# A linear-attention and token-mixing kernel whose whole schedule is written out in tables: all tables replaced, and zero products moved to the common pool of PSUM banks

## The chip, the cores and the metric

The kernel runs on one core of one Trainium2 chip. The metric is the device time of one execution in microseconds (us). Runs of one kernel agree within about 0.2%.

The engines are named as the profile names them: PE (TensorE, matrix products; PEld its weight loads), DVE (VectorE), ACT (ScalarE), POOL (GpSimd), SP (SyncE, which only issues DMAs here). DMAs are issued by SP, by ACT and by POOL, and run on 16 DMA engines.

## What is computed

```python
# attention, 4 batches, 8 heads, 768 steps, head size 48
for t in range(S):
    cur = np.einsum('bhd,bhe->bhde', u[None] * kt, vt)
    y[:, :, t] = np.einsum('bhd,bhde->bhe', rt, state + cur)
    state = w[None, :, :, None] * state + np.einsum('bhd,bhe->bhde', kt, vt)
# mixer on x = y as (4, 768, 384)
h = np.maximum(xt @ w_tok1, 0.0) @ w_tok2     # xt: steps and channels swapped; 256 hidden
u = x + h.transpose(0, 2, 1)
out = u + np.maximum(u @ w_ch1, 0.0) @ w_ch2  # 1536 hidden
```

All inputs and the output are float32; the products run in bfloat16 with float32 sums.

## The kernel before

**Chunks.** Each batch's 768 steps are cut into six chunks of 128. For a chunk, k and r are scaled by powers of the decay (tables `wnat`, `wp`, `wpair`, made once on ACT), turned (k on PE or by a DMA transpose; r in a "window" of two chunks for batches 0 and 1), and multiplied to scores `at_ps`. DVE masks the scores into `AT` (two masks of 128x512 a chunk). PE adds `AT` times v, and r times the state so far, in `y_ps`; the term of u (the "own" term: u*k*r summed per head into `adg`, times v) is added at the end, and the result goes to `x_b`. The state moves on in `kv_ps` and `S`. Batches 2 and 3 take their four inputs' products and the own term on POOL alone, five operations a chunk.

**Mixer.** When a batch's six chunks are in `x_b`, one task takes the hidden products `h_ps<-x_b,wtok`; then come the way back (`hT_ps`, or `hx_ps` with a turn on PE for three of the first four half batches), the turned `uT`, 24 "up" products `z_ps` (two half batches of 12, three products of 384 columns each), a relu each into `zr` on ACT or DVE, and "down" products `h_ps<-wch,zr`, in tasks of four, whose sums go to `osb` and are stored. The MLP of one batch is the work that PE does while the attention of the next batch is prepared on the other engines.

**Weights.** Seven loads by POOL, with a cast to bfloat16: w0 (`w_tok1`), w1 (`w_tok2`), w2 (the first third of `w_ch1`, for up products 0 to 3 of 12), w3 (the other two thirds, of double size), w4, w5, w6 (thirds of `w_ch2`).

**What sets the order.** Nothing is decided at run time. `add` (L208 and on, class `Plan`) numbers 908 tasks in the order in which the code creates them; `Plan.run` (L233) emits them in the order of `ORDER` (L21). Each engine works its own tasks in just that order (`InOrder`, L276; this is why the profile gives L282 to nearly every instruction), and waits in place for what a task needs. So the tables fix:

- `ORDER`: the queue of each engine, SP's and POOL's DMAs too;
- `BUFS` (L62): which buffer each tile takes; `m` are the seven PSUM banks of the common pool, `kv` the eighth;
- `ENGINES` (L151): for each task that can run on two engines, which one;
- `W_DEP` (L162): weight load i is issued only after a named load of (batch, chunk, input) landed; input 0 is k, 1 is r (of two chunks in batches 0 and 1), 2 is v;
- `HOLD` (L163): a load waits for another load's landing, which limits how many are under way; `GATES` (L176): a load waits for the landing of a weight load;
- `NWARM` (L177), `FILL` (L181): products with a zero tile `warm`, whose result nobody uses. Twelve of 512 columns are tasks of their own (`keep_warm`, L1189) and write the `kv` bank; five more are put by `fill` (L308) in front of the products of four tasks, in the bank which that task is about to fill.

Tasks that the text below speaks of: 44 (`t_uw`, L465: u times ones at 8 partitions, after two small DMAs on ACT, 4 and 5; PE's `turn_u`, 45, needs it); 28 to 36 and 50 to 52 (decay tables on ACT, L444); 16 and 17 (`mask2`, `place`); 119 to 125 (w0 to w6); 255 (the first up product); 333 on (batch 1), 531 on (batch 2), 711 on (batch 3); 774 and 782 (r products of batch 3's chunks 4 and 5, after whose transposes, 775 and 783 on SP, PE takes the scores, 785); 796 (the hidden products of batch 3).

Of the kernel before, what the change touches and what calls it, by code (L numbers as in the profile page):

```python
# [60 lines left out]
]  # L61
BUFS = {  # L62
    'AT0': [
    0, 1, 2, 0, 1, 0, 2, 1, 0, 2, 1, 0, 2, 1, 0, 1, 2, 1, 0, 2, 1, 0, 2, 1,
],
    'AT1': [
    0, 1, 2, 0, 1, 0, 2, 1, 0, 2, 0, 1, 2, 1, 0, 1, 2, 0, 1, 2, 0, 1, 2, 0,
# [8 lines left out]
    0, 0, 0, 0,  # L76
],
    'adg': [
    0, 1, 2, 3, 4, 1, 0, 2, 3, 4, 1, 0, 2, 3, 4, 0, 1, 2, 3, 0, 4, 1, 2, 3,
],  # L80
    'h1r': [
    0, 1, 0, 1,
# [41 lines left out]
    0, 1, 2, 3, 4, 0, 1, 2, 3, 0, 4, 2,  # L124
],
    'uT': [
    0, 1, 2, 3, 1, 0, 3, 2,
],
    'u_sb': [
    0, 1, 2, 3, 0,  # L130
# [1104 lines left out]
```

## Time and profile before

| | us |
|---|---|
| median of 3 runs | 163.41 (163.26 to 163.44) |
| the profiled execution | 163.55 |
| its span, from the first to the last instruction | 161.8 |
| PE, DVE, ACT, POOL busy in the span | 153.7, 114.1, 68.3, 85.7 |
| products PE `h_ps<-wch,zr` x300 | 54.0 |
| products PE `z_ps<-uT,wch` x288 | 52.0 |
| zero products `kv_ps<-warm` x12 | 5.2 |

The busy time of PE is that of overlapping products, whose ends are modelled. The chain of work that ended last follows the last instruction back to what released it, step by step. In rows of waits, the columns are the time in total, the number and the longest; in timelines, start, length, engine, operation, and in brackets the idle time before with what ended it.

### The profile page before, as it was taken

The numbers are of one execution on the slowest core, as the hardware profiler recorded it, in microseconds if no ns is written. First come the engines' busy times: TensorE is split into PE (matmuls) and PEld (weight loads), VectorE is DVE, ScalarE is ACT, GpSimd is POOL, SyncE is SP. The second block draws the span as 40 slices with busy tenths as digits, with TensorE's granted clock in tenths as the row PEclk, the third lists the DMA queues.
The fourth block names the chain that finished last, engine by engine and source line by source line (L and its number), as shares of the span: only waits on it lengthen the run. The fifth ranks groups of instructions, "written<-read, shape, count | busy, mean of one in ns | idle before, by whom it ended". The sixth has DMA issues, their size and how long they took to land.

```text
span 161.8 us, 3784 instructions
## 1 busy us (share of the span) xinstructions
PE 153.7 (95%) x1459; PEld 102.2 (63%) x1459; DVE 114.1 (70%) x243; ACT 68.3 (42%) x153; POOL 85.7 (53%) x108
## 2 busy tenths in 40 slices
PE   6998789899999899999999999999999999999992
PEld 1465567567666677666677765677666666666671
DVE  6689874568888998598799927967899245743423
ACT  3989785727732441246146341046541202242200
POOL 7149892008581179999959895999924000000000
PEclk9999999999999999999999999999999999999999
DMA  4999899998989899999999799898990143500133
GB/s 126 202 205 182 138 236 222 209 231 165 231 153 221 177 203 175 239 199 145 199 237 203 173 234 169 169 233 177 170 267 21 48 88 131 150 26 0 44 142 106
DMA packets 93061, 26.89 MB, mean 166 GB/s; under 512 B 87794, under 2 KB 92148, under 8 KB 93044
## 3 DMA queue, kind: packets, MB, share of 16 engines
q1 hardware_dynamic: 90688, 23.40, 70.6%
q0 software_dynamic: 2160, 3.15, 11.3%
q8 instruction: 11, 0.18, 0.5%
q10 hardware_dynamic: 196, 0.11, 0.2%
q14 instruction: 6, 0.05, 0.1%
HBM read 20.46 MB, written 4.72 MB: 156 GB/s over the span
## 4 chain that ended last, share of the span: by engine, by line
PE 65%; DMA 22%; DVE 3%; ACT 3%; SPq 2%; issue 1%; POOL 1%; POOLq 0%
PE h_ps L282 30%; PE z_ps L282 24%; DMA wch<-in_moe_w_ch_dram 9%; DMA kt<-in_k_dram 8%; DMA vt<-in_v_dram 5%; PE hT_ps L282 3%; PE y_ps L282 3%; PE at_ps L282 3%; SPq L282 2%; DVE AT L282 2%; PE kv_ps L282 1%; PE hx_ps L282 1%; DVE S L282 1%; ACT vb L282 1%; POOL kr L282 1%
## 5 line engine op out<-in xcount | busy, mean ns | idle before, releaser
L282 PE MATMUL h_ps<-wch,zr 128*128 128x384 bf16 (+1 forms) x300 | 54.0, 319 | 0.7 <-DMA wch<-in_moe_w_ch_dram 0.5
L282 PE MATMUL z_ps<-uT,wch 128*128 128x384 bf16 x288 | 52.0, 326 | 0.6 <-DMA wch<-in_moe_w_ch_dram 0.6
L282 ACT ACTIVATE zr<-z_ps 128x384 bf16<-128x384 f32 x59 | 27.6, 494 | 46.8 <-PE z_ps L282 39.4
L282 PEld LDWEIGHTS <-wch 128*128 128x128 bf16 x288 | 31.4, 114 | 13.8 <-DMA wch<-in_moe_w_ch_dram 1.0
L282 PEld LDWEIGHTS <-zr 128*128 128x128 bf16 x300 | 27.3, 97 | 16.0 <-issue 0.7
L282 DVE TENSOR_TENSOR AT<-at_ps,mask 128x512 bf16<-128x512 f32 x48 | 31.1, 683 | 5.4 <-PE at_ps L282 5.2
L282 DVE TENSOR_SCALAR zr<-z_ps 128x384 bf16<-128x384 f32 x37 | 19.6, 552 | 10.6 <-PE z_ps L282 9.5
L282 POOL TENSOR_TENSOR kr<-kt,wnat 128x384 bf16<-128x384 f32 x19 | 18.9, 1003 | 3.2 <-DMA kt<-in_k_dram 2.5
L282 POOL TENSOR_TENSOR yd<-vb,adg 128x384 f32<-128x384 bf16 x15 | 12.4, 834 | 8.7 <-DVE adg L282 3.9
L282 DVE TENSOR_TENSOR osb<-u_sb,h_ps 128x384 f32<-128x384 bf16 (+1 forms) x16 | 8.2, 525 | 10.7 <-PE h_ps L282 10.4
L282 PEld LDWEIGHTS <-kr 128*128 128x128 bf16 x176 | 12.0, 103 | 5.6 <-POOL kr L282 2.2
L282 ACT CAST vb<-vt 128x384 bf16<-128x384 f32 x19 | 9.6, 512 | 8.7 <-DMA vt<-in_v_dram 8.7
L282 POOL TENSOR_TENSOR rku<-ku,rt 128x384 f32<-128x384 f32 x12 | 12.0, 1012 | 1.0 <-DVE adg L282 0.9
L282 POOL TENSOR_TENSOR kr<-rt,wp 128x384 bf16<-128x384 f32 x12 | 12.2, 1036 | 0.0
L282 POOL TENSOR_TENSOR kr<-win,wpair 128x384 bf16<-128x384 f32 x4 | 4.9, 1230 | 13.5 <-DMA win<-in_r_dram 13.5
L282 POOL TENSOR_TENSOR ku<-kt,u_bc 128x384 f32<-128x384 f32 x12 | 12.0, 1009 | 0.0
L282 DVE TENSOR_TENSOR x_b<-y_ps,yd 128x384 bf16<-128x384 f32 x18 | 9.6, 549 | 2.1 <-PE y_ps L282 1.8
L282 PEld LDWEIGHTS <-wtok 128*128 128x128 bf16 x78 | 7.4, 98 | 4.3
L282 DVE TENSOR_TENSOR u_sb<-x_b,hT_ps 128x384 bf16<-128x384 bf16 x15 | 7.7, 549 | 3.4 <-PE hT_ps L282 3.4
L282 PE MATMUL h_ps<-x_b,wtok 128*128 128x384 bf16 x48 | 8.8, 326 | 0.0
L282 PE MATMUL y_ps<-vb,AT 128*128 128x48 bf16 x192 | 8.7, 183 | 0.0
L282 PEld LDWEIGHTS <-AT 128*128 128x128 bf16 x192 | 7.1, 96 | 0.3
(96 smaller groups left out, 181.8 us busy)
## 6 DMA issues: line engine op xcount, KB each, us to landing
kt<-in_k_dram SPq DMA_DIRECT2D x24, 192.0 KB, 4.1
vt<-in_v_dram SPq DMA_DIRECT2D x24, 192.0 KB, 3.7
out_dram<-osb SPq DMA_DIRECT2D x23, 192.0 KB, 2.5
win<-in_r_dram SPq DMA_DIRECT2D x6, 384.0 KB, 5.2
rt<-in_r_dram SPq DMA_DIRECT2D x12, 192.0 KB, 3.6
wch<-in_moe_w_ch_dram POOLq DMA_DIRECT2D x4, 384.0 KB, 6.6
wtok<-in_moe_w_tok_dram POOLq DMA_DIRECT2D x2, 384.0 KB, 5.6
wch<-in_moe_w_ch_dram POOLq DMA_DIRECT2D x1, 768.0 KB, 11.3
```

Of the source, the lines that this page charges most:

```text
L282: return lambda *args, **kw: tc.keep_in_program_order(f(*args, **kw))
```

## The change

Every table is replaced: `ORDER`, `BUFS` (with the same numbers of buffers), `ENGINES`, `W_DEP`, `HOLD`, `GATES`. `FILL` and the function `fill` go. Twenty-two zero products, of 512 or 256 columns, are tasks of their own and take banks of the common pool, like any other product; before, twelve of 512 columns wrote the `kv` bank. The arithmetic is the same.

```diff
 ORDER = [
-    0, 3, 22, 54, 18, 6, 16, 8, 896, 42, 59, 21, 897, 43, 39, 23, 53, 7, 13, 24, 19, 9, 2, 14, 56, 1, 11, 17, 4, 898,
...
+    3, 9, 56, 15, 10, 18, 53, 43, 7, 0, 22, 8, 58, 896, 46, 13, 19, 39, 54, 897, 11, 24, 12, 2, 20, 42, 23, 21, 14, 1,
+    898, 25, 899, 33, 900, 66, 32, 901, 31, 902, 130, 59, 903, 6, 166, 30, 132, 146, 5, 168, 4, 61, 126, 148, 133,
+    904, 905, 55, 127, 218, 128, 906, 129, 907, 64, 162, 908, 909, 910, 44, 163, 169, 45, 911, 63, 182, 134, 164, 47,
...
-W_DEP = [(0, 2, 2), (0, 5, 0), (0, 5, 0), (0, 3, 2), (1, 2, 0), (1, 1, 2), (1, 5, 0)]
+W_DEP = [(0, 3, 0), (0, 3, 2), (0, 4, 2), (0, 5, 2), (1, 2, 1), (1, 0, 2), (1, 4, 0)]
-HOLD = {(0, 4, 1): (0, 2, 1),
...
+HOLD = {(0, 5, 0): (0, 0, 0),
+        (0, 2, 1): (0, 2, 0),
+        (0, 3, 0): (0, 0, 1),
+        (0, 0, 2): (0, 5, 0),
+        (0, 4, 1): (0, 2, 1),
+        (0, 4, 0): (0, 3, 0),
+        (0, 1, 2): (0, 0, 2),
+        (0, 2, 2): (0, 4, 1),
         (0, 3, 2): (0, 4, 0),
+        (0, 4, 2): (0, 1, 2),
+        (1, 0, 1): (0, 2, 2),
         (0, 5, 2): (0, 3, 2),
+        (1, 0, 0): (0, 4, 2)}
-GATES = {(2, 0, 2): 1, (2, 4, 1): 3, (3, 1, 0): 2, (3, 1, 1): 6, (3, 5, 2): 5}
+GATES = {(1, 1, 0): 2, (1, 2, 2): 5, (2, 1, 2): 6}
-NWARM = 12
+WARM = [
+    512, 256, 512, 512, 512, 512, 512, 256, 512, 512, 512, 512, 512, 512, 512, 512, 256, 512, 512, 512, 512, 256,
 ]
-FILL = {138: 2, 154: 1, 159: 1, 190: 1}
...
     def keep_warm(cols):
         def f():
-            fresh = bank[0] is None
-            if fresh:
-                new_bank("kv0")
-            pe.matmul(bank[0][:, 512 - cols:512], warm[:, 0:128], warm[:, 0:cols], start=fresh or cols == 512, stop=True,
-                      skip_group_check=True)
+            pe.matmul(ps("warm_ps", [128, 512])[:, 0:cols], warm[:, 0:128], warm[:, 0:cols], start=True, stop=True)
         return f
 
-    for i in range(NWARM):
-        add("PE", "warm", keep_warm(512 if i in WIDE_AT else 128), [t_warm])
+    for cols in WARM:
+        add("PE", "warm", keep_warm(cols), [t_warm], take=("m",))
```

Read per engine, the two orders differ as follows (b is the batch, c the chunk):

| queue | before | after |
|---|---|---|
| SP, first loads | r window 0 and 1, k0, k1, r window 2, v1, k3, k2, k4, v0, v2, v3, v4, k5, v5 | k1, k0, k2, r window 0, k5, r window 1, k3, v0, r window 2, k4, v1, v2, v3, v4, b1 r window 0, v5 |
| ACT, first tasks | DMAs 3 and 6, function table, DMAs 4 and 5, ln, nine decay tables | DMA 3, function table, ln, three decay tables, DMA 6, one table, DMAs 5 and 4; the other tables later |
| DVE before task 255 | 57 tasks: 12 wide products, 6 score products, 12 masks, 3 state or `uT` copies, `place` | 54 tasks: 8, 5, 12, 8 copies (state, `x_b`, `uT`), task 44 before the second half of window 1 |
| POOL around the weights | two tables, w0, c0 and c2 own, k5, w1, c3 and c4 own, w2, w3 | k3, w0, three products and a table, c1 and c0 own, c4's u product, c2 own, w1, w2, c4 and c3 own, w3 |
| POOL from batch 1's first product to 774 or 782 | 64 entries | 77 entries |
| POOL behind that | five products, four own | two products, four own |
| PE, last five tasks (four products each) | 891, 883, 892, 888, 893 | 883, 887, 892, 888, 893 |

Between tasks 255 and 434 (the hidden products of batch 1), 434 and 616 (of batch 2), and 616 and 796, PE has the same kinds and numbers of tasks in both, but for one that moves across.

More of the change, by code (lines that the diff above doesn't have):

```diff
@@ L63 @@
     'AT0': [
-    0, 1, 2, 0, 1, 0, 2, 1, 0, 2, 1, 0, 2, 1, 0, 1, 2, 1, 0, 2, 1, 0, 2, 1,
+    0, 1, 2, 0, 2, 1, 0, 2, 1, 0, 2, 0, 1, 2, 0, 2, 1, 2, 0, 2, 1, 2, 0, 1,
 ],
     'AT1': [
-    0, 1, 2, 0, 1, 0, 2, 1, 0, 2, 0, 1, 2, 1, 0, 1, 2, 0, 1, 2, 0, 1, 2, 0,
+    0, 1, 2, 0, 2, 1, 0, 2, 1, 0, 2, 1, 0, 2, 1, 0, 2, 0, 1, 2, 0, 1, 2, 1,
 ],
@@ L78 @@
     'adg': [
-    0, 1, 2, 3, 4, 1, 0, 2, 3, 4, 1, 0, 2, 3, 4, 0, 1, 2, 3, 0, 4, 1, 2, 3,
+    0, 1, 2, 3, 4, 1, 2, 0, 4, 3, 1, 2, 4, 0, 3, 1, 2, 4, 3, 0, 1, 4, 2, 3,
 ],
@@ L84 @@
     'kp': [
-    0, 1, 2, 3, 4, 5, 0, 1, 4, 2, 3, 0, 4, 5, 1, 2, 0, 3, 5, 1, 4, 2, 0, 3, 5, 1, 2, 0, 4, 3,
+    0, 1, 2, 3, 4, 5, 3, 5, 0, 4, 5, 2, 1, 3, 0, 4, 1, 5, 2, 3, 5, 0, 1, 4, 3, 2, 0, 1, 5, 4,
 ],
     'kt': [
-    0, 1, 2, 3, 4, 5, 0, 1, 2, 3, 4, 5, 0, 1, 2, 3, 4, 5, 0, 2, 1, 3, 4, 5,
+    0, 1, 2, 3, 4, 5, 1, 2, 0, 3, 4, 5, 1, 2, 0, 3, 4, 5, 2, 3, 0, 1, 4, 5,
 ],
     'ku': [
-    0, 1, 2, 0, 1, 0, 2, 0, 1, 2, 0, 1,
+    0, 1, 2, 1, 0, 2, 1, 0, 2, 1, 0, 2,
 ],
@@ L96 @@
     'm': [
[7 rows of a table removed]
[8 rows of a table added]
 ],
     'osb': [
-    0, 1, 2, 0, 1, 2, 2, 1, 0, 1, 2, 2, 0, 1, 2, 0, 1, 0, 2, 0, 1, 2, 0, 1, 2,
+    0, 1, 2, 0, 2, 0, 2, 0, 1, 2, 1, 1, 2, 1, 0, 1, 2, 1, 1, 0, 2, 1, 0, 2, 1,
 ],
     'pr': [
-    0, 1, 1, 0, 1, 0, 1, 0, 1, 0, 1, 0,
+    0, 1, 1, 1, 0, 1, 0, 1, 0, 1, 1, 0,
 ],
     'rk': [
-    0, 1, 2, 3, 0, 1, 2, 3, 1, 0, 2, 3,
+    0, 1, 2, 3, 0, 1, 2, 3, 1, 0, 3, 2,
 ],
     'rka': [
-    0, 1, 2, 0, 1, 2, 0, 1, 2, 0, 1, 2,
+    0, 1, 2, 0, 1, 2, 0, 2, 1, 0, 2, 1,
 ],
@@ L120 @@
     'rku': [
-    0, 1, 1, 0, 1, 1, 0, 1, 0, 1, 0, 1,
+    0, 1, 1, 1, 1, 0, 1, 0, 1, 0, 0, 1,
 ],
     'rt': [
-    0, 1, 2, 3, 4, 0, 1, 2, 3, 0, 4, 2,
+    0, 1, 2, 3, 4, 0, 3, 2, 1, 4, 0, 3,
 ],
     'uT': [
-    0, 1, 2, 3, 1, 0, 3, 2,
+    0, 1, 2, 3, 0, 1, 3, 2,
 ],
@@ L132 @@
     'vb': [
-    0, 1, 2, 3, 4, 0, 1, 3, 2, 4, 0, 1, 3, 2, 4, 3, 1, 0, 2, 3, 4, 1, 0, 3,
+    0, 1, 2, 3, 4, 1, 0, 2, 4, 3, 1, 0, 2, 3, 4, 0, 1, 3, 2, 4, 0, 1, 3, 4,
 ],
     'vt': [
-    0, 1, 2, 3, 4, 5, 0, 1, 3, 2, 4, 5, 0, 1, 3, 2, 5, 4, 0, 3, 1, 2, 4, 5,
+    0, 1, 2, 3, 4, 5, 0, 1, 2, 3, 4, 5, 0, 1, 2, 3, 4, 5, 0, 1, 2, 3, 4, 5,
 ],
     'win': [
-    0, 1, 2, 1, 0, 2,
+    0, 1, 2, 0, 1, 2,
 ],
     'yd': [
-    0, 1, 2, 0, 2, 1, 0, 2, 1, 2, 0, 2, 0, 1, 2, 0, 1, 2,
+    0, 1, 2, 0, 1, 2, 0, 1, 2, 0, 1, 0, 2, 1, 0, 1, 2, 0,
 ],
@@ L147 @@
     'zr': [
-    0, 1, 2, 1, 0, 2, 1, 0,
+    0, 1, 2, 0, 1, 2, 0, 1,
 ],
@@ L189 @@
 NKP = 6
-LATE = [0, 1]
+LATE = [
+    0, 1,
+]
 GROUPS = [[(0,), (1,), (2,), (3,), (4,), (5,)], [(0,), (1,), (2,), (3,), (4,), (5,)], [(0, 1), (2, 3), (4, 5)],
@@ L306, in mul @@
         engine_of[on].tensor_mul(out, a, c)
-    def fill(bank, fresh):
-        for i in range(FILL.get(plan.now, 0)):
-            pe.matmul(bank, warm[:, 0:128], warm[:, 0:bank.shape[-1]], start=fresh, stop=True, skip_group_check=True)
     EITHER = {"ACT": "copy384p", "DVE": "x384p"}
@@ L606, in add_state @@
                 kv[0] = bank[0][:, 0:dm].rearrange("p (a q d) -> p a q d", a=HP, q=2)
-                fill(bank[0][:, 0:dm], True)
-            else:
-                fill(bank[0][:, 0:dm], False)
-            if g == 0:
                 if c > 0 and not carried:
@@ L778, in outputs @@
                 y_ps = L["y"] = ps("y_ps", [128, dm])
-                fill(y_ps, True)
                 start = True
@@ L795, in add_own @@
             def add_own():
-                fill(L["y"], False)
                 for j in range(2):
@@ L946, in outputs @@
             y_ps = L["y"] = ps("y_ps", [128, dm])
-            fill(y_ps, True)
             start = True
@@ L1020, in f @@
                     begin()
-                fill(M["h1"][0], cs[0] == 0)
                 for c in cs:
```

15 lines of the change are left out of this document (removed), and 108 rows, old and new, of tables (BUFS, ENGINES, ORDER).

## The prediction

> **What bounds the kernel now.** I read the utilisation slices first, then busy time by stage, then the chain of work that ended last, then the waits, and last the GpSimd and DMA timelines.
>
> ```profile
> span 161.8 us, 3784 instructions
> PE   6998789899999899999999999999999999999992
> DMA  4999899998989899999999799898990143500133
> GB/s 126 202 205 182 138 236 222 209 231 165 231 153 221 177 203 175 239 199 145 199 237 203 173 234 169 169 233 177 170 267 21 48 88 131 150 26 0 44 142 106
> ```
>
> The page's slices: PE looks nearly full from the second slice on, and the DMA engines are full from slice 2 to slice 29, some 120 us.
>
> ```profile
> 0.00:31.56 31.56, 27.48 (x293) 16.52 (x294) 23.06 (x64) 23.10 (x51) 17.56 (x35) 1.00 1.02 189
> 31.56:60.00 28.44, 27.49 (x302) 19.22 (x303) 23.65 (x49) 13.87 (x34) 13.07 (x14) 1.00 1.01 198
> 60.00:124.16 64.16, 64.10 (x642) 43.80 (x641) 51.42 (x101) 24.31 (x56) 54.58 (x59) 1.00 0.98 192
> 124.16:161.80 37.64, 34.65 (x224) 22.64 (x224) 15.95 (x32) 7.03 (x15) 0.49 (x1) 1.00 0.26 79
> ```
>
> Busy time by stage (PE, weight loads, DVE, ACT, POOL, then granted clock, DMA share, GB/s). Between 60.00 and 124.16 PE is idle for 0.06 us, and GpSimd is busy for 54.58 of 64.16. I cut at 31.56 and 124.16 because the chain does:
>
> ```profile
> 31.56 0.68 PE z_ps L282 x3
> 46.94 6.54 DMA wch<-in_moe_w_ch_dram
> 53.52 0.98 PE h_ps L282 x7
> 119.18 1.88 DVE AT L282 x3
> 124.16 4.72 PE h_ps L282 x28
> 135.87 3.90 PE z_ps L282 x24
> 152.93 5.89 PE h_ps L282 x48
> 158.85 0.35 DVE osb L282
> ```
>
> The chain (start, length). Before 31.56, where the first product of the channel MLP starts, it consists of loads and vector work; from 53.52 it is PE throughout, but for 119.18 to 124.16, where batch 3's last masks and states on VectorE lead to the last hidden product. 24 products in 3.90 us are 162.5 ns for 384 columns, so PE is at its pace there, while the same products show a "busy" of 326 ns. In the first stage "27.48 busy" is therefore no sign of a full array.
>
> ```profile
> PE z_ps L282 <- DMA wch<-in_moe_w_ch_dram: 0.6, 1, 0.6
> PE h_ps L282 <- DMA wch<-in_moe_w_ch_dram: 0.5, 1, 0.5
> PE trk L282 <- POOL kr L282: 0.3, 1, 0.3
> ```
>
> PE's waits from 30 to 60 us, all of them: 1.4 us; the view lists none from 60 to 160. So **the span is 31.56 us of a start that PE doesn't set, then 130.2 us (161.8 - 31.56) of product stream with little to win.** A schedule can gain in the start, and can lose wherever the stream is made to wait.
>
> **The change part by part.** The sums are made against the profiled execution, 163.55 us with a span of 161.8, 0.14 above the median of 163.41.
>
> *Zero products.* Five fills and twelve warm products go, 22 come (18 of 512 columns, 4 of 256).
>
> ```profile
> 3.84 3.59 PE L282 MATMUL kv_ps<-warm 128*128 128x512 bf16 x8
> 7.22 2.01 PE L282 MATMUL tr_ps<-ident,kr 128*128 128x128 bf16 x16
> ```
>
> Eight took 7.22 - 3.84 = 3.38 us, 423 ns each: half of the later pace (512 columns by 162.5/384 are 217 ns), though the granted clock reads 1.00. The new first eight run in this same empty time, and the next eight while PE waits for the first r window. Six (2,560 columns, 1.1 us) stand between batch 0's own products, where PE is half empty; I cost them at nothing, 1.1 us if that cover is gone and minus nothing, since the clock is already up by then. Taking banks of the common pool adds a wait for the reader of that bank; what waits behind is all of PE's queue, but only in the start. The Trainium skill, "TensorE: Matmul & The Clock Gate", Part 1, says that the array runs at half rate until it was busy for about 3.4 us, and that this ramp is under 1% of a usual span. The rows agree (half rate until about 7.2 us); by that rule ten products more could bring 1.6 us at most, and I give them none.
>
> *The start.* What sets 31.56?
>
> ```profile
> 4.00 0.31 ACTq L282 DMA_DIRECT2D wp<-in_u_dram  x1
> 7.93 0.57 POOL L282 TENSOR_TENSOR wp<-wp 8x128 f32<-8x128 f32 x1 [3.63 <-DMA wp<-in_u_dram]
> 17.14 1.02 POOL L282 DMA_DIRECT2D wtok<-in_moe_w_tok_dram  x1
> 23.82 1.65 POOL L282 DMA_DIRECT2D wch<-in_moe_w_ch_dram  x2
> 37.10 2.27 POOL L282 TENSOR_TENSOR kr<-win,wpair 128x384 bf16<-128x384 f32 x2 [11.63 <-DMA win<-in_r_dram]
> 26.39 0.33 PE L282 MATMUL y_ps<-ydb,ident 128*128 128x384 bf16 x1
> 1.94 5.26 DMA kt<-in_k_dram
> 7.28 3.72 DMA vt<-in_v_dram
> 11.01 3.00 DMA kt<-in_k_dram
> 14.03 4.64 DMA vt<-in_v_dram
> 23.82 7.69 DMA wch<-in_moe_w_ch_dram
> ```
>
> (Timelines, then the chain.) Each held load starts when an earlier one lands, a hop of 3.00 to 4.64 us, 3.8 in the mean. The new HOLD takes batch 0's last v over four hops (r window 0, k of chunk 3, k of 4, v of 3, v of 5). The first four loads are 960 KB, as were the three that had landed by 7.20 (1.94 + 5.26); four hops from there give 22.4. Now it leaves at 18.67 (14.03 + 4.64) and takes one hop: 22.5. The loads alone bring nothing. VectorE has less to do before the first z: eight wide products for twelve and no `place`, but eight x, state and transposed copies for three. It also gets a **new wait**: the u product moves from GpSimd to VectorE, and its two small DMAs go behind four tables on ACT (about 7.6 us instead of 4.00). By the 3.9 us from 4.00 to 7.93 it can start at 11.5; behind it in VectorE's queue stand the second half of window 1 and every mask of batch 0, and PE's queue waits with them (turn_u, then the scores). VectorE is free for it at about 10.2 (window 1 landed, one product done), so 1.3 us are lost, nothing at best. After it come twelve masks at 0.63 (the chain's 1.88 for three) and fifteen others at 0.36 (23.06 for 64 in the first stage), 13.0 us: 24.5, and with 1.3 of waits 25.8. From the last own term on PE to the first z it takes 31.56 - 26.39 less the 0.6 waited for weights, 4.6 us, so z starts at **30.4**. The weights must be there too: w2 leaves at 23.82 now and takes 7.69 to 31.51. It goes ahead of two own terms on GpSimd, but behind a product that needs chunk 4's transposes; I put its issue at 22 to 24, and batch 1's second k is gated on its landing, so less competes: 29.5 to 31.5. First z: 30.4, ends 29.3 and 33. **Term: -1.2 us.**
>
> *PE's waits after it (1.4 us).*
>
> ```profile
> wch<-in_moe_w_ch_dram POOLq DMA_DIRECT2D x1, 768.0 KB, 11.3
> ```
>
> w3 (the page's DMA issues: 11.3 us to landing), for the later two thirds of the up products, leaves GpSimd after both own terms, about 26, one later than now. Eight up products (3.9 us) cover until 34.3; with less beside it I put its landing at 34 to 36, so up to 1.5 us may be lost, and 3 if it takes 11.3 again. w4 still waits for batch 1's second r window (at 37.10 now), which the gate lets leave only when w2 has landed, but no longer for its two products (2.27 us); the 0.5 us may go or stay. Taken: 1.4 as before, ends 0 and 3.
>
> *Batches 2 and 3, GpSimd.* The largest risk.
>
> ```profile
> 56.14 1.16 POOL L282 TENSOR_TENSOR pr<-rka,rkb 128x512 bf16<-128x512 bf16 x1 [6.78 <-ACT rka L282]
> 75.69 1.62 POOL L282 TENSOR_TENSOR yd<-vb,adg 128x384 f32<-128x384 bf16 x2
> 107.73 3.90 POOL L282 TENSOR_TENSOR kr<-rt,wp 128x384 bf16<-128x384 f32 x4
> 111.56 1.02 POOL L282 TENSOR_TENSOR rku<-ku,rt 128x384 f32<-128x384 f32 x1
> 108.77 5.50 SPq L282 DMA_TRANSPOSE rk<-kr  x4
> 118.52 0.62 PE L282 MATMUL at_ps<-rk 64*128 64x128 bf16 x16
> ```
>
> A product has a pitch of 0.96 us ((111.56 - 107.73)/4), an own term 0.79. The last r product of batch 3 ends at 111.56, the last of the four transposes leaves near 112.9 (108.77 and three times 5.50/4) and, at a hop of 4, lands near 117; PE reaches the scores at 118.52: 1.5 us of slack. From the first batch-1 product at 37.10 to 111.56 GpSimd handles 64 entries, some 60 us at these pitches, and idles 14 (6.78 of it at 56.14). After the change the stretch has 77: fifteen new (three window halves, four products and three own terms of batch 1, mask2, one table, three batch-3 products that moved ahead), two gone, together 13 us more at 1.14, 0.96, 1.16 and 0.79 by kind. But it begins after w3, at 26.6, not 37.10: 10.5 us earlier. With the same idle it ends at 114.1; without the 6.78 wait (that product moves to VectorE) but with new waits on gated loads I put idle at two less, and the end at 112. The transposes then go out as they come, 0.4 later, where four queue up now: 112.4 against 112.9. Cost nothing; ends -1.5 and +3.
>
> *The tail* has the same order of products, sums and stores: nothing.
>
> **Sum:** -1.2; span 160.6, or 163.41 - 1.2 = **162.2 us** at the median.
>
> **The rivals.** (A) *Bigger gain*: w2 lands early, w3 does not stall, GpSimd is ready: first z at 29.6 and 0.7 of waits gone, -2.6: 160.8. For it: 1.4 us of waits are there to go; against: batch 3's VectorE chain at 119.18 must move as well. 0.16. (B) *Nothing*: z starts earlier and stops at w3, since DMA is full to 120 us either way: 163.4. 0.10. (C) *Slower, GpSimd late*: 13 us of moved work reach its end. It decides from the point at which the last r product of batch 3 ends after 114.0 (112.9 now, less 0.4 for the issue, plus 1.5 of slack); each microsecond beyond costs one. With idle at 16 us (the 14 of now and two on gated loads): end 116.1, +2.1, 165.5. For it: 54.58 of 64.16 busy. Against: the long wait at 56.14 goes. 0.25. (D) *Slower, in the start*: w0 leaves at 12, not 17.14, in the middle of the loads. The weights' queue (w0 to w6, w3 of double size) took 11.3% of 161.8 us for eight parts:
>
> ```profile
> q0 software_dynamic: 2160, 3.15, 11.3%
> ```
>
> 18.3/8 = 2.3 us, all of it ahead of chunk 5's v: first z at 32.7, +1.1, 164.5. The Trainium skill, "DMA: Bandwidth & Descriptors", Issuing engines are not separate DMA queues, speaks for it: transfers of all queues share the same 16 engines and interleave. Against: slices 3 and 4 moved 182 and 138 GB/s, so there is room. 0.13. That tables judged by a model do not hold on the chip would look like C or D. My forecast has 0.36, for 161.4 to 163.0.
>
> **How the numbers follow.** This kernel's measurement tells 0.2% (0.33 us) from nothing. Faster is forecast and A, 0.52; same 0.10; slower C and D, 0.38. The range leaves half of A (0.08) below 160.8 and the longer half of C (0.12) above 165.4.
>
> **What would show it.** First z at 29.3 to 31 and the u product on VectorE waiting near 10 to 11.5 for a DMA; PE waits of 30 to 60 us near 1.4 and none later; GpSimd's last r product of batch 3 before 113; the last hidden product 37.6 us before the end (161.80 - 124.16), as now. Wrong if scores of batch 3 wait for transposes (C), or batch 0's v lands after 24 (D).

## The result: 6 us slower, and the profile after

The changed kernel takes 169.38 us (168.47 to 170.06) beside 163.43 before, 1.036 times as long (95% interval 1.030 to 1.043). One of the four executions of the kernel before took 170.15 and is left out of the ratio. The profiled execution took 170.06, with a span of 168.4 against 161.8. Its page, first lines and slices:

```profile
span 168.4 us, 3778 instructions
PE   5979991999959998999999999999999999999992
PEclk9999999699999999999999999999999999999999
DMA  5999999999999999168999999999994027112043
```

Each digit stands for 4.21 us. PE has a hole in slice 7 (from 25.3 us) and half a hole in slice 12 (46.3), and right behind the first hole the granted clock reads 0.6. Before, the clock row was all nines. The stages, cut where the chain cuts them, as before (PE, weight loads, DVE, ACT, POOL, clock, DMA share, GB/s):

```profile
0.00:35.87 35.87, 28.53 (x297) 17.37 (x298) 24.91 (x58) 18.52 (x43) 19.39 (x33) 0.95 1.04 193
35.87:60.00 24.13, 21.79 (x212) 15.05 (x210) 19.86 (x37) 12.01 (x27) 14.17 (x18) 1.00 1.02 181
60.00:130.89 70.89, 70.27 (x736) 48.28 (x734) 55.85 (x113) 29.89 (x68) 59.35 (x65) 1.00 0.92 178
130.89:168.40 37.51, 34.48 (x225) 22.53 (x222) 17.82 (x37) 4.85 (x11) 0.00 (x0) 1.00 0.26 80
```

The chain passes through z from 35.87 on; the first z product of all starts at 35.71 instead of 31.56, 4.2 us late. The rest takes 132.7 us (168.4 - 35.71) instead of 130.2, another 2.5. The tail is the same (37.5 us, 37.6 before). PE's waits between 20 and 75 us, all of them, and five pieces of the chain (start, length):

```profile
PE y_ps L284 <- DVE vb L284: 3.7, 1, 3.7
PE tr_ps L284 <- DVE zr L284: 2.1, 1, 2.1
PE at_ps L284 <- DVE pr L284: 0.5, 1, 0.5
```

```profile
21.53 4.50 DMA vt<-in_v_dram
26.52 2.81 DVE vb L284
30.55 1.28 PE h_ps L284 x4
43.98 2.77 DVE place L284 x2
118.15 1.00 POOL kr L284
```

No wait for weights is left (1.1 us of the 1.4 before), and three waits for VectorE stand in their place. Behind the two long ones is an operation that copies from SBUF to SBUF. (The third, 0.5 us, comes behind a cast at 63.14 that took 0.92 beside an own term of GpSimd.) The same cast in the kernel before, then VectorE's timeline in the changed one, then GpSimd's beside it:

```profile
24.89 0.35 DVE L282 CAST vb<-vt 128x384 bf16<-128x384 f32 x1
```

```profile
26.52 2.80 DVE L284 CAST vb<-vt 128x384 bf16<-128x384 f32 x1 [1.56 <-DMA vt<-in_v_dram]
43.98 3.62 DVE L284 COPY place<-ident 64x64 bf16<-64x64 bf16 x4
```

```profile
26.31 0.81 POOL L284 DMA_DIRECT2D wch<-in_moe_w_ch_dram  x1 [1.43 <-DMA vt<-in_v_dram]
27.14 1.95 POOL L284 TENSOR_TENSOR kr<-win,wpair 128x384 bf16<-128x384 f32 x2
43.39 0.60 POOL L284 DMA_DIRECT2D wch<-in_moe_w_ch_dram  x1
44.01 1.97 POOL L284 TENSOR_TENSOR kr<-kt,wnat 128x384 bf16<-128x384 f32 x2
45.93 0.59 POOL L284 DMA_DIRECT2D wch<-in_moe_w_ch_dram  x1
```

Read the ends, not the starts. The cast of chunk 5's v took 2.80 us and ended at 29.32, 0.2 after GpSimd's two products (29.09). Before the change it took 0.35: there GpSimd was issuing w2 and w3 too (23.82 to 25.47), but had nothing behind them until 37.10. The four copies of `place`, 0.8 us in the kernel before, took 3.62; the first alone took 2.67 and ended at 46.65, right behind the issue that began at 45.93. The new table starts w3's issue upon the landing of the same v that the cast waits for, and puts `place` (which nothing reads, since no window is paired) into the middle of the product stream. Then the clock:

```profile
25.87:29.28 3.41, 0.00 (x0) 0.00 (x0) 2.76 (x1) 0.90 (x3) 2.76 (x3) 1.00 1.22 205
29.28:32.70 3.42, 3.32 (x23) 2.06 (x23) 0.80 (x3) 0.48 (x1) 1.00 (x1) 0.50 1.11 206
32.70:36.11 3.41, 3.41 (x36) 2.55 (x35) 2.27 (x5) 1.27 (x4) 0.00 (x0) 1.00 1.19 242
```

These are windows of 3.41 us, the grid on which the clock's records change in this trace. PE did nothing in the first; in the next it got half the clock while it was busy for 0.97 of it, which costs at most 3.41 x 0.5 x 0.97 = 1.6 us. Four hidden products took 1.28 us there, and 0.65 in a kernel below (e1_no_place) that had full rate at that point. From chunk 5's own term on PE (30.18) to the first z (35.71) it took 5.5 us here and 4.4 there, so some 1.2 us are the half rate's.

**First theory:** VectorE's copies are held by GpSimd's runs, and the hole that this makes halves PE's rate. **Rivals:** the last v, which landed at 26.03 and not at 22.4, sets the start whatever the cast does (case D of the prediction); or GpSimd is late for batch 3 (C). C can be put aside: the second r product of batch 3's last pair ran to 119.15, 49.2 us before the end of the span (50.2 before the change). The chain does pass through GpSimd from 117.19 to 129.07, by that product and the last own terms, but PE idles 0.6 us in all between 60.00 and 130.89, 0.5 of them behind the cast at 63.14.

### The profile page after: what moved, and what is told of

It reads as the page before. It is cut to its first block, busy times and chain, and to the rows that moved or that the text cites. A ratio compares the mean times of both kernels' runs of the same rounds, so it can differ in the third digit from the quotient of the medians.

```text
span 168.4 us, 3778 instructions
## 1 busy us (share of the span) xinstructions
PE 155.1 (92%) x1464; PEld 103.2 (61%) x1464; DVE 118.4 (70%) x241; ACT 65.3 (39%) x149; POOL 92.9 (55%) x115
## 3 DMA queue, kind: packets, MB, share of 16 engines
q0 software_dynamic: 2160, 3.15, 11.5%
## 4 chain that ended last, share of the span: by engine, by line
PE 62%; DMA 16%; DVE 10%; issue 4%; POOL 4%; SPq 1%; POOLq 0%; ACT 0%; DVEq 0%
PE h_ps L284 31%; PE z_ps L284 17%; DMA vt<-in_v_dram 6%; DMA kt<-in_k_dram 5%; PE y_ps L284 4%; PE hT_ps L284 3%; PE hx_ps L284 3%; DMA win<-in_r_dram 3%; DVE zr L284 3%; PE at_ps L284 2%; DVE place L284 2%; DVE vb L284 2%; DMA rt<-in_r_dram 2%; POOL yd L284 1%; PE kv_ps L284 1%
## 5 line engine op out<-in xcount | busy, mean ns | idle before, releaser
L284 PEld LDWEIGHTS <-wch 128*128 128x128 bf16 x288 | 31.6, 114 | 13.2 <-issue 0.2
L284 ACT ACTIVATE zr<-z_ps 128x384 bf16<-128x384 f32 x55 | 25.1, 492 | 37.0 <-PE z_ps L284 36.7
L284 PEld LDWEIGHTS <-zr 128*128 128x128 bf16 x300 | 27.4, 98 | 15.5 <-issue 0.4
L284 DVE TENSOR_SCALAR zr<-z_ps 128x384 bf16<-128x384 f32 x41 | 21.7, 552 | 15.3 <-PE z_ps L284 15.0
L284 POOL TENSOR_TENSOR yd<-vb,adg 128x384 f32<-128x384 bf16 x18 | 14.9, 839 | 12.1 <-ACT vb L284 4.8
L284 POOL TENSOR_TENSOR kr<-kt,wnat 128x384 bf16<-128x384 f32 x18 | 18.3, 1026 | 3.7 <-DMA kt<-in_k_dram 3.7
L284 PEld LDWEIGHTS <-kr 128*128 128x128 bf16 x176 | 11.0, 100 | 6.6 <-issue 2.6
L284 ACT CAST vb<-vt 128x384 bf16<-128x384 f32 x21 | 10.7, 515 | 9.6 <-DMA vt<-in_v_dram 9.5
L284 POOL TENSOR_TENSOR kr<-win,wpair 128x384 bf16<-128x384 f32 x9 | 9.2, 1038 | 5.4 <-DMA win<-in_r_dram 5.3
L284 PE MATMUL h_ps<-x_b,wtok 128*128 128x384 bf16 x48 | 9.8, 351 | 0.0
```

Source lines behind the costliest of these rows:

```text
L284: return lambda *args, **kw: tc.keep_in_program_order(f(*args, **kw))
```

## The experiments

Every profiled execution can be split at its first z product, and the two parts turned out to answer to different edits (the last three rows are variants of the kernel before and of g1_best):

| kernel | first z | from there to the end | span | `place` | half rate before the first z |
|---|---|---|---|---|---|
| before | 31.56 | 130.2 | 161.8 | 0.8, at 3.8 us | none |
| changed | 35.7 | 132.7 | 168.4 | 3.62 | 29.3 to 32.7 |
| e1_no_place | 33.9 | 130.5 | 164.4 | - | 14.1 to 20.9 |
| e2_v5_act | 33.1 | 130.7 | 163.8 | 1.81 | 16.8 to 20.2 |
| e3_w0_late | 33.9 | 133.1 | 167.0 | 3.78 | 14.5 to 21.4 |
| e4_all | 35.7 | 130.3 | 166.0 | - | 30.3 to 33.8 |
| f1_fill | 32.9 | 132.8 | 165.7 | 3.80 | 16.6 to 20.0 |
| f2_u_later | 31.9 | 132.8 | 164.7 | 3.78 | 15.5 to 18.9 |
| f3_mended | 32.3 | 130.1 | 162.4 | - | 16.1 to 19.5 |
| g1_best | 32.2 | 129.4 | 161.6 | - | none |
| h1_two_edits | 32.9 | 130.4 | 163.3 | - | none |
| i1_w3_later | 32.2 | 133.3 | 165.5 | 3.91 | none |
| g2_place_mid | 31.5 | 130.8 | 162.3 | 1.24, at 38.8 us | none |
| h2_before_no_fill | 31.7 | 129.8 | 161.5 | as before | 11.2 to 21.5 |
| h3_u_loads | 33.8 | 130.0 | 163.8 | - | none after 12.6 |

Executions of one kernel differ by whether and where a window falls to half rate, so times scatter, and ratios have wide intervals.

**One edit at a time.** `place` left out:

```diff
-ORDER: ... 297, 367, 17, 299 ...
+ORDER: ... 297, 367, 299 ...
```


> The changed kernel without the fill of `place` (a memset and four 64x64 copies on VectorE, which nothing reads); everything else as it is. Theory 1 (port): VectorE operations that copy from SBUF to SBUF wait until a run of GpSimd work ends; `place` at 43.98 was held for 3.62 us by it, and the relus behind it kept PE idle for 2.1 us. Without it that gap goes: 169.4 falls to 166.8 to 167.5. Theory 2 (late loads) and theory 3 (GpSimd late in batch 3): nothing but `place`'s own 0.8 us on an engine with room, 169.0 to 169.4, and PE idles the 2 us elsewhere.

Measured: 166.21 us median, ratio to before 1.010 (0.996 to 1.025). The wait of 2.1 is gone from PE's list, and the second part is 130.5. The four executions were 163.79 at full rate, 166.11 and 166.31 with a mean clock of 0.98, and 170.12 with 0.97; one window at half rate takes 0.01 off that mean (1.7 of 165 us). So with this one edit the execution in which no window fell is within 0.4 us of the kernel before; it is a single one, and in this kernel's profile the cast was hardly held either (0.74 us).

The cast on ScalarE:

```diff
-ENGINES[55]: 1
+ENGINES[55]: 0
```


> The changed kernel with the cast of batch 0's last v on ScalarE instead of VectorE. Theory 1 (port, then clock): the cast takes 0.5 us right behind the landing at 26.0 instead of 2.80, the array's gap of 3.7 us shrinks to under 1.2, the granted clock stays at 1.00 between 29 and 34, first z near 31.9 instead of 35.87: 165.2 to 165.8. Theory 2 (only the late landing counts, the cast would be hidden or the clock lost anyway): first z at 35.0 or later, 168.5 or more.

Measured: 169.11 median; the profiled execution took 165.53, with first z at 33.1. The wait for the cast was gone, and chunk 5's own term on VectorE (two operands in SBUF) waited in its place, 0.96 us instead of 0.56. An earlier window, 13.4 to 16.8, held little work and was followed by half rate to 20.2; between 29 and 34 the rate was full, as the theory had it. The profiled time is the expected one, the other three (168.89 to 170.85) are not. Inconclusive by its times.

w0 later:

```diff
-ORDER: ... 165, 119, 57 ... 40, 147 ...
+ORDER: ... 165, 57 ... 40, 119, 147 ...
```


> The changed kernel with the issue of w0 moved in GpSimd's queue from 12.97 to about 17.2 (behind the first table product, ahead of the own terms). Theory 2 (w0 in the middle of the hops delays batch 0's last two v): v of chunk 3 needs 3.8 us instead of 6.36, the last v lands near 23.0 instead of 26.03, 166.0 to 167.0. Theory 1 alone (GpSimd's w3 and window products start upon the same landing as the cast): the landing may move but the cast still takes 2.8, the gap is shorter only by what the landing gains; if the loads are bound by bandwidth the landing stays at 26 and the time at 169.4.

Measured: 169.66, ratio 1.036 (1.024 to 1.048): no gain. The v of chunk 3 did go through in 3.0 us (issued 15.03, next issue 17.99) instead of 6.36, and the cast came at 27.46 all the same, behind chunk 5's masks, which two windows at half rate (14.5 to 21.4) had made late. e1_no_place, with w0 where the table puts it and half rate in the same place, has the same cast (27.47) and the same first z. So with half rate there the loads don't set the start; what they do without it this run does not show.

> All three together, `mask2` left out as well (read by nothing), and the cast of batch 1's chunk 4 on ScalarE too. Theory 1 and 2 both: first z 30 to 31, no gap at 46, 161.3 to 162.5, below the kernel before (163.43). Theory 1 alone: 162.5 to 163.3. Theory 3 (GpSimd's chain in batch 3 is the bound by then): 164.5 or more, with PE idle between 112 and 128.

(Those three edits, `mask2` (task 16) out as well, and the cast of batch 1's chunk 4 on ScalarE.) Measured: 168.35, ratio 1.030 (1.018 to 1.042): no better than `place` alone. With the cast out of the way, the own term on VectorE took 2.12 us beside the same two products (27.46 to 29.58), and the window behind it fell to half rate. The stall had moved one instruction down the queue. All theories missed the time.

**The zero products and the u product.**

```diff
-    for cols in WARM:
-        add("PE", "warm", keep_warm(cols), [t_warm], take=("m",))
+    for i, cols in enumerate(WARM):
+        add("PE", "warm", keep_warm(cols, 7 if i == 14 else 1), [t_warm], take=("m",))
```
(`keep_warm` issues its product that many times.)

> The changed kernel with six more zero products of 512 columns (1.3 us at full rate) behind the last one ahead of the transpose of u, where the array waits 1.2 to 1.9 us. Clock theory (a window of 3.4 us with the array under about 0.4 busy halves the rate for the next one): no half rate between 14 and 21 us in any phase of the windows; the one after the gap at 25.7 to 29.4 stays when the cast is held: 167.5 to 169.4, with less scatter. Rival (the zero products only stand in the way): 169.4 or more.

Measured: 167.61, ratio 1.023 (1.017 to 1.029). The window that held them kept the work up (0.87 of what PE can do), the next one, 13.2 to 16.6, did not, and half rate followed at 16.6 to 20.0, which the theory had ruled out. The median is 1.8 us better than the changed kernel's; the scatter did not shrink (166.70 to 172.98).

```diff
-ORDER: ... 910, 44, 163, 169, 45, 911 ... 164, 47, 138 ...
+ORDER: ... 910, 163, 44, 169, 911 ... 164, 138, 45, 47 ...
```


> The changed kernel with the product of u behind the second half of window 1 in VectorE's queue, and its transpose behind window 1's transposes and chunk 0's scores in PE's. If the new wait (1.3 us in the prediction) costs: chunk 5's masks end 1.0 to 1.5 us earlier, and where v has landed the first z too: 167.9 to 168.5. If the last v (26.03) and its cast decide alone: 169.4, and the gap at 25.7 only begins earlier, with half rate after it.

Measured: 170.52 median, 166.44 in the profiled execution, whose first z is the earliest of the single edits (31.9 against 32.9 of f1_fill with as much half rate). So the new wait seems worth about 1 us there, by one execution of each, and the times do not show it.

**All mends**, then with four more zero products at 12.8 us and a later k of batch 1 (besides what is shown: f2_u_later's edit, `mask2` and `place` out, and two casts on ScalarE as in e4_all):

```diff
-ORDER: ... 202, 143 ... 189, 214, 228, 224, 219, 122, 216 ... 225, 237 ...
+ORDER: ... 202, 119, 143 ... 189, 224, 219, 214, 228, 216 ... 225, 122, 237 ...
-ENGINES[59]: 1
+ENGINES[59]: 0
```


> The changed kernel with all mends: `place` and `mask2` left out (read by nothing), the product of u later as above, w0 issued behind chunk 4's k product, chunk 5's cast on ScalarE ahead of chunk 4's state and its own term on GpSimd ahead of w3 and the window products, batch 1's chunk 4 cast on ScalarE. Port, late loads and the new wait together: first z 30.3 to 31.5 and full rate throughout: 161.3 to 162.8, under the kernel before (163.4). If the start has another bound (weights, masks): first z 32 or later, 163.5 to 165.

Measured: 164.07 (163.32 to 164.74, ten executions), ratio 1.005 (1.0025 to 1.007). 5.3 of the 6 us are back, and the scatter with them: own term on GpSimd ahead of w3, cast on ScalarE, `place` out. The first z, 32.3, did not reach the 30.3 to 31.5 expected: the last v landed at 25.4 (issued 19.22, while w0, issued at 17.30, was under way to 22.77), and one window was still at half rate.

```diff
+    add("PE", "warm", keep_warm(512, 4), [t_warm], take=("m",))
-        (1, 0, 0): (0, 4, 2)}
+        (1, 0, 0): (0, 5, 2)}
```


> The mended kernel with four more zero products of 512 columns behind the transpose of u (into a bank whose readers have ended), where its own window of 3.4 us had the array 0.47 busy and the next ran at half rate, and batch 1's first k held until batch 0's last v has landed. If the clock window and the landing at 25.4 hold the first z at 32.3: full rate from 9 us on in nearly all executions, last v at 23 to 24, first z 30.8 to 31.5: 162.3 to 163.3, under the mended kernel (164.07) and at or under the kernel before (163.4). Rival (w2's landing near 30.8 or the masks are the bound): first z as before, 163.8 to 164.5.

Measured: ratio to before 1.0008 (0.997 to 1.0045). Of twelve executions five took 163.0 to 163.4, four 164.2 to 164.8, three longer (one 200.59, at a mean clock of 0.76). The profiled one had full rate throughout, as expected, but the first z stayed at 32.2. The last v landed at 24.6, 6.5 us after its issue (w0 under way from 17.00 to 23.88), but the chain to the first z does not pass through it: it runs over chunk 5's own term, w3's issue and the two window products on GpSimd, to 29.63. No version beat the kernel before; this one equals it.

**The reverse:** `place` late in the kernel before.

```diff
-ORDER: ... 11, 17, 4 ... 274, 368, 260 ...
+ORDER: ... 11, 4 ... 274, 368, 17, 260 ...
```


> The kernel before with one thing changed: the fill of `place` (five instructions, 0.9 us) moves in VectorE's queue from 3.6 us to the relu at 38.44, where GpSimd has products, an issue and an own term in a row from 37.10 to 40.84. Port theory: the four copies need 1.5 to 3.5 us instead of 0.82, the relus behind come late, 0.5 to 2.5 us slower. Rival (the 3.62 us had another cause): 0.82 us, same time within 0.3.

Measured: ratio 1.003 (0.9998 to 1.006), so about +0.5 us, which is not clear of noise. The copies took 1.24 instead of 0.8, only the first was held (0.75), and PE got a new gap of 1.3 us at 39.4. Here a product and not an issue was in progress when the copy asked.

**What holds a copy?** Four kernels that only run VectorE against GpSimd.

> A kernel that computes nothing of the reference (its output is a constant): VectorE runs one operation while GpSimd runs n products of 128x384 (about 0.96 us each) back to back, started about 0.9 us before it. Theory 1 (the operation gets the port only when GpSimd's run ends): the cast from SBUF to SBUF takes 0.35 to 0.42 us alone, near 0.5 with n = 1, 1.5 with 2, 3.4 with 4 and 7 with 8; the strided 64x64 copy and a product of two SBUF operands the same; a cast out of PSUM stays at 0.4 to 0.55. Rival (handed over at each instruction): 1.4 at most for any n. Rival (no such link, the 2.8 us came from elsewhere): 0.42 throughout.

The first theory fell: with runs of 1 to 8 products the cast took 0.36 to 0.43 (0.78 once, where it came earlier in a product), and the strided copy 0.93 where it came early in one. A cast out of PSUM took 0.55 beside four products, no more than the same cast with GpSimd idle. But these products waited for each other (pitch 1.07), so gaps could explain it.

> A kernel that computes nothing of the reference: one VectorE operation against runs of GpSimd products in the form of this kernel (128x384 into bf16, a tile each, so that they follow without a gap) and DMA issues, with four offsets of the request. In the first such kernel each product waited for the one before it (pitch 1.07) and the cast came in at the first end. Theory (it comes in only where GpSimd leaves a gap): up to 1, 2, 3 and 6 products are waited for. Rival (at the end of the instruction in progress): never over 1.1 us. Third (at most the one in progress and those already taken up): 1 to 2 instructions, whatever the length of the run.

Without gaps the same: never over 0.70 for the cast, 0.54 for the copy and 0.90 for a product of two SBUF operands, whatever the length of the run. Each ended 0.1 to 0.4 behind the end of the GpSimd product in progress. That is what the Trainium skill, "SBUF — State Buffer", Who interferes with whom, states: of VectorE (copying in a fast mode, or reading two SBUF operands) and GpSimd the one that issues first holds the shared port for its whole instruction, and the other blocks. The 2.8 us of the changed kernel stay unexplained by it.

> A kernel that computes nothing of the reference: a cast on VectorE against four GpSimd products in a row, or a product, a DMA issue of the size of w3 and two products, with the request 0.05 to 0.95 us into the instruction in progress, in steps of 0.03. If an early request misses the first end (the next instruction had been taken up before it): casts of 1.9 us and more at small offsets, and at most 1.0 at large ones. If it comes in at the first end wherever it falls: never over 1.3 us, and the 2.8 us of the changed kernel stay open.

The offset doesn't matter: 0.03 us into a product the cast took 1.18 and ended where all others did. In the two timelines, VectorE's and GpSimd's, the four products beside it start at 25.45:

```profile
25.49 1.18 DVE L47 CAST castT<-src 128x384 bf16<-128x384 f32 x1
```

```profile
25.45 3.96 POOL L47 TENSOR_TENSOR kr<-ga,gb 128x384 bf16<-128x384 f32 x4 [0.60 <-DVE gb L47]
```

What was left untried was a request during a DMA issue with products queued behind it, which is what both held operations of the changed kernel had met.

> A kernel that computes nothing of the reference: a cast on VectorE requested at sixteen points, 0.03 us apart, inside or just around a DMA issue of GpSimd (of the size of w5) that is followed without a gap by two products, another issue and a product. If a request that falls into an issue is not served at its end but only behind the products (as `place` at 43.98 and the cast at 26.52 in the changed kernel): casts of 2.3 to 3.2 us for requests inside the issue, under 1.1 for those before it. If it is served at the issue's end: never over 1.1.

```profile
9.45 3.09 DVE L47 CAST castT<-src 128x384 bf16<-128x384 f32 x1
```

```profile
9.23 0.59 POOL L47 DMA_DIRECT2D big<-in_moe_w_ch_dram  x1
9.84 1.95 POOL L47 TENSOR_TENSOR kr<-ga,gb 128x384 bf16<-128x384 f32 x2
11.73 0.59 POOL L47 DMA_DIRECT2D big<-in_moe_w_ch_dram  x1
```

All sixteen casts, thirteen asked during the issue and three within 0.1 us of its end, took 2.62 to 3.09 us and ended 0.2 behind the next issue: both products went first. The cast at 9.45 asked 0.22 into the issue and ended at 12.54. The first copy of `place` shows the same in five kernels (the changed one, e3, f1, f2, i1: 2.67 to 2.87 us): issue, two products, issue, then the copy. That page of the Trainium skill tells of DMA issues only as the side that a copy of VectorE starves.

It is not the whole rule. These casts asked during w3's issue (e1_no_place, from 27.15 to 27.96) and when no issue was in progress (i1_w3_later, 0.06 us before the end of an own term):

```profile
27.47 0.74 DVE L284 CAST vb<-vt 128x384 bf16<-128x384 f32 x1
```

```profile
24.90 2.19 DVE L284 CAST vb<-vt 128x384 bf16<-128x384 f32 x1
```

The first ended right behind the issue, with products next in the queue, as did those of e3_w0_late, f1_fill, f2_u_later and h1_two_edits (0.74 to 0.86 us). The second waited for two products without any issue. Chunk 5's own term asked 0.27 us into the first window product in e4_all and in h1_two_edits; it took 2.12 us in one, behind two products, and 1.16 in the other, behind one. And the cast of the kernel before, asked during w3's issue with nothing queued behind, took 0.35. So an issue alone does not hold the copy; products beside it or behind it do, and what decides how many of them go first stays open.

**The clock by itself.**

> A kernel that computes nothing of the reference: stretches of 14 us in which the array does k = 1, 2, 3, 4, 6 products of 512 columns, then waits about 0.7 us for ScalarE (busy 0.24, 0.38, 0.48, 0.55, 0.65), and stretches of dense products with 64, 32 and 1 rows, and 32 and 8 columns of the array; 40 dense ones between. If busy time decides with a bound near 0.4: half rate for k = 1 and perhaps 2, full from 3 on, full in the dense ones. If the share of the rows in use counts too: half rate for 32 rows and 1 row as well.

Windows of that kernel (the granted clock is the third figure from the end): one product, then a wait; two and a wait; three and a wait; dense with 64 rows; with 32 rows; with one row; with 8 columns. The second is the last one at full rate of its stretch, from 44.7 to 58.3 the clock reads 0.50.

```profile
20.78:24.20 3.42, 1.76 (x3) 0.31 (x3) 0.00 (x0) 1.40 (x4) 0.00 (x0) 0.50 0.00 0
41.26:44.68 3.42, 1.56 (x6) 0.57 (x6) 0.00 (x0) 1.44 (x3) 0.00 (x0) 1.00 0.00 0
68.57:71.98 3.41, 1.80 (x7) 0.57 (x6) 0.00 (x0) 1.24 (x3) 0.00 (x0) 1.00 0.00 0
136.84:140.25 3.41, 3.41 (x17) 1.50 (x16) 0.00 (x0) 0.00 (x0) 0.00 (x0) 1.00 0.00 0
164.14:167.56 3.42, 3.42 (x9) 1.18 (x8) 0.00 (x0) 0.00 (x0) 0.00 (x0) 0.50 0.00 0
198.27:201.69 3.42, 3.42 (x10) 1.17 (x8) 0.00 (x0) 0.00 (x0) 0.00 (x0) 0.50 0.00 0
250.00:253.41 3.41, 3.41 (x18) 1.35 (x17) 0.00 (x0) 0.00 (x0) 0.00 (x0) 1.00 0.00 0
```

PE is "busy" for 3.42 of 3.42 us with 32 rows, at half rate (0.43 us from product to product); with 64 rows, or with 8 columns, it keeps full rate (0.216). So the rows in use count, times time, and the columns don't. Counting each product by its length (0.216 us for 512 columns streamed, at full rate) and its rows of 128, the windows of all these traces line up: those followed by half rate held 0.00 to 0.36 of the work that PE can do in one, those that kept it 0.32 or more; in between both happened. The kernel before has 0.44 in its emptiest. Once at half rate, by the same count, 0.32 and less left it there, and 0.39 and more brought full rate back (as shares of the window's time, in which each product then takes twice as long, 0.64 and 0.78). The bound is about the same both ways if work is what counts; if time is what counts, coming back takes more. The runs don't tell.

The window's grid isn't tied to the kernel (its first boundary stood at 1.8 to 3.2 us in some executions, at 0.3 to 1.0 in others), so whether a weak stretch fills a whole window differs from execution to execution.

> The kernel before without its five fills and two of its twelve warm products (1.2 us of array time between 15 and 20 us). The windows of 3.41 us there hold 0.44 to 0.54 of the array's work; without them about 0.25 to 0.35. Clock theory: half rate for one window in most executions, 164.5 to 167. As the prediction had it (zero products cost and bring nothing once the clock is up): 163.2 to 163.6.

(`FILL = {}`, tasks 906 and 907 out.) Measured: half rate for three windows in eight of ten executions, by their mean clocks; from 11.2 to 21.5 in the profile:

```profile
PEclk9985589999999999999999999999999999999999
```

and 163.39 us beside 163.37, ratio 0.9988 (0.9955 to 1.002). A miss for the theory: half rate came and cost nothing that shows. The chain to the first z ends, as in the kernel before, in w2's load (23.74 to 31.61; 23.82 to 31.51 before). Half rate has a price where PE has work waiting, as at 29.28 in the changed kernel.

**What is left.**

```diff
-ORDER: ... 367, 17, 299 ...
+ORDER: ... 367, 299 ...
+    add("PE", "warm", keep_warm(512, 3), [t_warm], take=("m",))
```


> The changed kernel with two edits only: the fill of `place` left out (read by nothing), and eight more zero products of 512 columns between 10.7 and 15 us (five behind the last one ahead of the transpose of u, three behind chunk 0's scores). If `place` (2.3 us) and the half rate in the start make most of the loss: 163.8 to 165.5, and full rate in most executions; what is left is the held cast. If the cast, the late v or w0 matter by themselves: 166 to 167.5 at full rate.

(And six zero products for one at task 910.) Measured: 165.55, ratio 1.012 (1.007 to 1.017), full rate in four of six executions. `place`, the half rate and the longer hold of the cast (0.81 us here) are then about 4 of the 6 us; 2 stay, with the u product, w0 and the own term (1.16 beside a product) where the table puts them.

```diff
-ORDER: ... 219, 122, 216 ... 333, 230, 36, 233, 231, 334, 240 ...
+ORDER: ... 219, 216 ... 333, 230, 36, 233, 231, 334, 122, 240 ...
```


> The changed kernel with one move: w3's issue goes behind the two products of batch 1's window 0 in GpSimd's queue. `place`, the product of u, w0 and the cast on VectorE stay. If the cast was held by the issue and what follows it, and the half rate came of that gap: the cast ends by 27.3 instead of 29.3, the gap at 25.7 is under 2 us, full rate from 29 on, first z 32.5 to 34: 166.0 to 167.5. If the late v sets the start: first z 35.5, 169 to 170.

Measured: 170.16 median. In the profiled execution (167.23, full rate, 1.024 times the kernel before) the first z came at 32.2, 3.5 earlier than in the changed kernel and a little earlier than expected; the cast was still held, by the two products (2.19 us), but from 24.9 on, so that PE's hole was 1.5 and its window stayed full. The other three executions, with mean clocks of 0.98 to 0.99, took 170.0 to 172.4, and the ratio, 1.046 (1.037 to 1.055), is theirs. The trace shows the shorter gap and the full rate behind it; the edit is no mend.

> The mended kernel with three more zero products (instead of four) and u's two small loads and w's by head ahead of the tables on ScalarE, as in the kernel before. If the u product (11.49, then the transpose and chunk 2's scores) is what holds the start: scores of chunk 2 at 13.5 instead of 14.70, first z 31.0 to 31.7 instead of 32.2: 162.2 to 163.0, 0.3 to 0.8 under the kernel before. If the last v (landing at 24.6) holds it: 163.0 to 163.5, no different from before.

(Tasks 6, 5 and 4 ahead of task 25 in ScalarE's queue.) Measured: 166.88, ratio 1.022 (1.017 to 1.026), worse than without. The logarithm of w had been at 4.42 in g1_best and now came at 6.35, behind the two loads; all tables followed, PE idled 1.8 us at 6.8, and its first full rate began at 12.6. That the table had put these loads late was worth what it cost.

## Why the prediction was wrong

**The step that failed is the start, "Term: -1.2 us"**, which measured +4.2, and within it the sentence "After it come twelve masks at 0.63 ... and fifteen others at 0.36". Among these others is chunk 5's cast: 2.80 us, for which the profile of before had no row, since there no product of GpSimd stood beside it. The same blindness is in "VectorE has less to do before the first z: ... (no `place`)": I took `place` off the start and never asked where it went. It went to 43.98, beside a GpSimd run, and cost 2.1 us of PE's time in the product stream, for which the prediction had nothing. I had listed what moved ahead on GpSimd as a load on GpSimd alone, and not as something that VectorE shares a port with.

The forecast's first z was 30.4 and the measured one 35.7. An estimate from the rows shown: VectorE was to be done at 25.8, with PE's own term next; PE's own term came at 30.18, 4.4 later. Of these, 2.4 are the hold (2.80 against 0.35), and 1.9 the late v, without whose landing the cast could not ask before 26.52. From there PE took 5.5 instead of 4.6, 0.9 more, at half rate. The masks themselves were done at 24.96, before the 25.8. That 25.8 holds an error of its own: the 1.3 us of waiting for u had already moved the sum's beginning from 10.2 to 11.5 and were added once more.

Point by point:
- *Zero products, "the clock is already up by then".* It was up by then (from 9.85 in the kernel before, by the trace's first record of full rate, and not from "about 7.2"), and went down again behind the hole (1.2 us, 1.6 at most). The page of the Trainium skill that I had cited for the ramp ("TensorE: Matmul & The Clock Gate", Part 1) also says that an idle window of about 3.4 us brings half rate back; the trace agrees (empty 25.87 to 29.28, half rate behind it), and I had not asked which later gap might fill one. Taken alone (h2), the removal costs nothing that shows.
- *The new wait of the u product*, at 10 to 11.5 by 1.3 us: it waited until 11.42, VectorE idled 0.7 us and PE 1.0 for it, and f2_u_later puts its price near 1 us, by one execution. Right in kind, a little smaller.
- *The last v at 22.4*: it landed at 26.03. The mean hop of 3.8 us was too short: v of chunk 3 took 6.36 beside w0. That is rival D's mechanism, and the traces bear it out: from its issue to the next hop that v took 4.9 to 6.4 us in the seven kernels whose w0 was issued before it, and 2.8 to 4.0 in the five whose w0 came later (e3, e4, f3, g1, h3). e3 differs from the changed kernel in nothing else: 2.96 against 6.36. In f3 and g1 the later w0 met the last v instead, which took 6.2 and 6.5. The mark of D ("lands after 24") was met, and its price was put too low, at 1.1. It is still not the whole: g1_best lives with 24.6 and equals the kernel before.
- *PE's waits, 1.4*: none of them was left. w2 landed at 30.29 (forecast 29.5 to 31.5) and w3 at 34.02 (34 to 36), so the landings were right, and the 1.4 that was kept in the sum was none, since the first z came later than both.
- *GpSimd in batches 2 and 3, nothing*: right in its price. The last hidden product is 37.5 us before the end (forecast 37.6), though the last r product ended at 119.15 and not before 113: it is the first z that shifted, and PE did not wait for it.
- *Rivals.* D had a part of it, none had the hold. The time, 169.4, lies 4 us above the range's end: the range was built from rivals in which transfers or GpSimd are late, and none in which an engine is slowed by its neighbour.

The sum as the runs give it: the changed kernel at full rate and without `place` takes 163.8 to 166.0 (e1, h1), that is 0.4 to 2.5 above before for the u product, the late v, and the cast and the own term, which took 0.7 to 1.2 us there instead of 0.35 and 0.56. `place` adds about 2.2 (132.7 from the first z on in the changed kernel, 130.5 in e1_no_place): from there, the five kernels in which it is held for 3.6 us and more need 132.7 to 133.3, those without it 129.4 to 130.5; e2, where it took 1.81, needs 130.7. What is left of the 6 us, 1 to 3, is put down to one or two windows at half rate, 1.2 to 1.6 each where PE has work, and to the hold of the cast; by subtraction, not by an experiment.

## What to carry to other kernels

When a change moves work to GpSimd or makes it start earlier, list VectorE's operations that only touch SBUF (casts of loaded tiles, copies that fill constants, products of two SBUF tiles) in the stretch where GpSimd now runs. Price them at the end of GpSimd's product in progress at least, and at two products and an issue, up to 3 us, where an issue with products behind it is near. Then look at what PE does meanwhile: a hole of 3.4 us or a stretch of thin products may halve its rate for the next windows, and that costs only where work is queued. Look too at which small loads a large one is put beside: their hops doubled here. Dead constants are not free when a table may put them anywhere.

## What the runs showed of the hardware

- A VectorE cast from SBUF that asked while GpSimd was issuing a DMA with two products and another issue queued behind it, or within 0.1 us of that issue's end, waited over all of them: 2.62 to 3.09 us in sixteen of sixteen tries (m5_port). In m4_port, where it asked during a product with no issue just ahead, it waited for that product alone, at 0.03 us into it (1.18 us) as at 0.76 (0.45). In the kernels themselves both outcomes occur (0.74 to 0.86 us during an issue in five, 2.19 without one in i1_w3_later).
- PE's clock gate goes by rows times time in windows of 3.41 us: dense products on 32 rows ran at half rate (0.43 us for 512 columns), on 64 rows, or on 8 columns of the array, at full (0.216). It falls below about a third (0.32 to 0.36 of the work of a window at full rate).
- A load of 192 KB took 4.9 to 6.4 us with a weight load under way when it was issued, and 2.8 to 4.0 where the weight load was issued later (the v of chunk 3, from its issue to the next, twelve kernels).
- Half rate for 10 us in a start that loads and VectorE pace cost nothing that shows (163.39 against 163.37 us).
